# Attention scores and row maxima of two heads at a time as pairs of 64-row TensorE tiles, in a fused attention and FFN kernel

## The chip, the cores and the metric

One core of a Trainium2 chip. The metric is the device time of one execution in microseconds (us); the median of three runs of the kernel before is 858.36 us.

## The reference, cut to what matters

Attention with queries that are mean-pooled by two, and an FFN with a leaky activation behind it, all in float32:

```python
q_pool = q.reshape(B, H, S // 2, 2, D).mean(axis=3)      # B, H, S, D = 4, 8, 1152, 64
scores = np.matmul(q_pool, k.transpose(0, 1, 3, 2)) / np.sqrt(D)
scores = scores - np.max(scores, axis=-1, keepdims=True)
attn = np.exp(scores)
attn = attn / (np.sum(attn, axis=-1, keepdims=True) + 1e-09)
out = np.matmul(attn, v)                                  # 576 pooled queries in each of 32 heads
x = out.transpose(0, 2, 1, 3).reshape(B * S // 2, H * D)  # 2304 x 512
h = x @ w_in                                              # 512 -> 2048
g = np.maximum(h, 0.0) + alpha * np.minimum(h, 0.0)
return g @ w_out                                          # 2048 -> 512
```

## The kernel before, in words

**Order.** Every piece of work is a task for one engine with a planned cost and a priority; a list scheduler (`Scheduler`) writes the program of each engine out once, at build time. On the chip each engine takes its instructions in that order and waits on semaphores.

**Stages.** First the attention of 32 heads (to 453.5 us of the span), then the "low sweeps" (the first 5 of 16 blocks of the FFN's hidden units, in 8 blocks of 288 tokens, L474 with 288 columns), then the "high sweeps" (the other 11 blocks, 5 blocks of 460 or 464 tokens). The FFN's weights come as 64-bit floats and are converted by VectorE and ScalarE (five VectorE operations each, L386 to L422) as the work goes on; ten of the 32 half blocks of weights ahead of the last row maxima.

**Precision.** Numbers are split into a high part (type fp32r) and a low rest, and products are summed from high*high, high*low and low*high.

**One head of attention.** `head_prep` loads the keys twice, one copy under the other (64 + 64 partitions), and the summed queries likewise; `q1` holds high queries on partitions 0 to 63 and, from `q_low` (L739), low ones on 64 to 127, under which `k1` holds the high keys twice. One matmul with 128 rows so gives high*high plus low*high. `k2` holds low keys and a row of -1 (65 rows), `q2` high queries and the row maximum. The scores of a block of 128 keys and 288 queries are two matmuls (L983, L984) into one of three PSUM banks; ScalarE takes exp of each (L996). `head_max` finds the row maximum of the next head: 12 blocks of 128 queries and 384 keys (L911), two blocks to a double bank, one VectorE reduction over 768 columns for both (L927). The 64 queries that are left over (576 is 4.5 times 128) go as a block-diagonal tile `bd` against half keys `k3` (L892, L901). A TensorE transpose (L945) and a DMA bring the maxima into `q2`. Weighted values (L1024) are matmuls of plain float32, two 64-column tiles per key block, the two halves of the queries side by side. Sums of exp go over blocks: VectorE and GpSimd add blocks (L1009), TensorE sums what is left in 32-column tiles (L1046, per pair of heads, four parts per head for heads 0 to 11, two after), and `pair_end` normalises.

```python
pairs = [blocks[i:i + 2] for i in range(0, len(blocks), 2)]   # head_max: two blocks share a reduction
double[i] = (bank[i], bank[i + 1]), t                         # banks 3+4 and 5+6, for maxima alone
```

## Time and profile before

| what | value |
|---|---|
| timed runs | 858.26, 858.36, 858.57 us |
| profiled execution: its span, first to last instruction | 853.4 us |
| runs' median less that span | 4.96 us |
| TensorE busy | 841.0 us, 99% of the span, 5477 matmuls |
| VectorE busy | 583.0 us, 68% |
| ScalarE busy | 535.8 us, 63% |
| GpSimd busy | 193.1 us, 23% |
| first score matmul, last matmul of attention's sums | at 17.16 and at 453.51 us |

The profile gives no own total for the profiled execution beside its span; the 4.96 us lie outside the span. Matmuls overlap each other, so a busy TensorE is not yet TensorE at its pace: its pace is read from the starts of matmuls that follow each other.

### The profile page before, as it was taken

Reading aid. Unit: us, or ns where it says so; the run is one execution under the profiler, and the core shown is the slowest. Engines: PE = TensorE matmul, PEld = TensorE weight load, DVE = VectorE, ACT = ScalarE, POOL = GpSimd, SP = SyncE. Lnnn points to the kernel's source line nnn. Section 1 sums busy time; section 2 is a strip of 40 time slices with the busy share of each in tenths; the row PEclk is TensorE's granted clock in tenths of the full one; section 3 lists DMA queues with packets and bytes.
Section 4 is the critical chain, followed back from the end, with each engine's and each line's share of the span. In section 5 each row is a group of like instructions: output and inputs, shape, how many; then the busy total and the mean of one; then the engine's idle time right before and its main releaser. Section 6 shows DMA issues by size and latency. Waiting matters only on the chain.

```text
span 853.4 us, 14873 instructions
## 1 busy us (share of the span) xinstructions
PE 841.0 (99%) x5477; PEld 708.7 (83%) x5477; DVE 583.0 (68%) x897; ACT 535.8 (63%) x1295; POOL 193.1 (23%) x146
## 2 busy tenths in 40 slices
PE   8999999999999999999999999999999999999997
PEld 7777777767877877877879999998888888888886
DVE  7988999999989989989894699623332323322423
ACT  6888888889899899888764576534332233222321
POOL 4534333235534545534530000000000000000000
PEclk9999999999999999999999999999999999999999
DMA  8355754685565665643443867545330321300301
GB/s 299 113 132 148 231 163 143 213 230 151 152 175 124 178 157 142 169 119 95 113 117 116 252 208 246 169 136 167 88 90 4 100 76 44 89 1 1 90 0 46
DMA packets 71376, 112.74 MB, mean 132 GB/s; under 512 B 20779, under 2 KB 45958, under 8 KB 71302
## 3 DMA queue, kind: packets, MB, share of 16 engines
q1 hardware_dynamic: 69430, 104.12, 40.5%
q0 software_dynamic: 1872, 7.67, 5.2%
q8 instruction: 43, 0.70, 0.3%
q14 instruction: 31, 0.25, 0.1%
HBM read 92.65 MB, written 19.02 MB: 131 GB/s over the span
## 4 chain that ended last, share of the span: by engine, by line
PE 82%; DVE 9%; DMA 4%; ACT 3%; issue 1%; SPq 0%; DVEq 0%; ACTq 0%
PE bank L474 40%; PE bank L1024 13%; PE bank L983 9%; PE bank L984 8%; PE bank L911 7%; DMA wraw<-wt 3%; PE bank L1046 2%; DVE wbits L416 1%; ACT pa L996 1%; PE bank L892 1%; DVE bx L927 1%; DVE wbits L410 1%; DVE wmag L422 1%; PE bank L945 1%; DVE pa L1009 1%
## 5 line engine op out<-in xcount | busy, mean ns | idle before, releaser
L1009 POOL TENSOR_TENSOR pa<-pa,pa 128x576 f32<-128x576 f32 x116 | 170.4, 1484 | 226.3 <-ACT pa L996 208.9
L996 ACT ACTIVATE pa<-bank 128x288 f32<-128x288 f32 x576 | 201.7, 411 | 30.8 <-PE bank L984 25.7
L927 DVE TENSOR_REDUCE bx<-bank 128x2 f32<-128x768 f32 x194 | 175.9, 947 | 10.6 <-PE bank L911 9.4
L983 PE MATMUL bank<-q,k 128*128 128x288 f32 x576 | 169.2, 309 | 2.6 <-ACT pa L996 1.2
L984 PE MATMUL bank<-q,k 65*128 65x288 f32 x576 | 163.3, 297 | 0.0
L1024 PE MATMUL bank<-pa,vv 128*64 128x288 f32 x1152 | 149.2, 410 | 0.0
L1024 PEld LDWEIGHTS bank<-pa,vv 128*64 128x64 f32 x1152 | 78.8, 137 | 56.1 <-issue 7.2
L983 PEld LDWEIGHTS bank<-q,k 128*128 128x128 f32 x576 | 108.6, 189 | 14.1 <-ACT pa L996 4.7
L519 DVE TENSOR_TENSOR gw<-gs,gw 128x460 fp32r<-128x460 f32 (+1 forms) x55 | 35.1, 638 | 119.4 <-ACT gw L514 119.2
L514 ACT ACTIVATE gw<-gs 128x460 fp32r<-128x460 f32 (+1 forms) x55 | 32.4, 589 | 124.4 <-PE bank L474 115.2
L984 PEld LDWEIGHTS bank<-q,k 65*128 65x128 f32 x576 | 109.3, 190 | 0.0
L911 PE MATMUL bank<-k,q 128*128 128x384 f32 x372 | 96.2, 342 | 0.1
L474 PE MATMUL bank<-gw,wh 128*128 128x460 f32 (+1 forms) x320 | 93.4, 373 | 0.5
L474 PE MATMUL bank<-wlow,wh 128*128 128x460 f32 (+1 forms) x320 | 93.0, 371 | 0.0
L508 DVE SCALAR_TENSOR_TENSOR gs<-gs,nal 128x460 f32<-128x460 f32 (+1 forms) x55 | 38.4, 699 | 56.1 <-ACT gs L503 56.0
L498 ACT ACTIVATE gs<-bank 128x460 f32<-128x460 f32 (+1 forms) x55 | 30.2, 549 | 63.0 <-PE bank L474 62.2
L474 PEld LDWEIGHTS bank<-gw,wh 128*128 128x128 f32 x320 | 59.3, 188 | 9.5 <-DVE x L590 2.5
L474 PE MATMUL bank<-x,wlow 128*128 128x288 f32 x480 | 67.1, 295 | 0.0
L474 PE MATMUL bank<-gs,wlow 128*128 128x288 f32 x480 | 66.2, 296 | 0.6 <-DVE gs L519 0.6
L474 PEld LDWEIGHTS bank<-wlow,wh 128*128 128x128 f32 x320 | 60.1, 188 | 7.1
L474 PEld LDWEIGHTS bank<-gs,wlow 128*128 128x128 f32 x480 | 64.1, 188 | 2.1 <-DVE gs L519 1.4
L474 PEld LDWEIGHTS bank<-x,wlow 128*128 128x128 f32 x480 | 64.8, 188 | 0.5 <-issue 0.4
(101 smaller groups left out, 1204.2 us busy)
## 6 DMA issues: line engine op xcount, KB each, us to landing
kk<-kt SPq DMA_DIRECT2D x31, 576.0 KB
wraw<-wt SPq DMA_DIRECT2D x32, 512.0 KB
qs<-qt SPq DMA_DIRECT2D x19, 576.0 KB
vv<-vt SPq DMA_DIRECT2D x32, 288.0 KB
xs<-x SPq DMA_DIRECT2D x64, 144.0 KB
x<-xs SPq DMA_DIRECT2D x32, 288.0 KB
qs<-qt POOLq DMA_DIRECT2D x13, 576.0 KB, 8.0
r<-rrd SPq DMA_DIRECT2D x64, 72.0 KB
```

What stands on the lines that cost most here:

```text
L474: nc.tensor.matmul(out=ps[:, :n], lhsT=w[a, c // DMO][:, c % DMO:c % DMO + P], rhs=lo(hl), start=(first and i == 0), stop=(last and i == 2),)
L498: ACT, act(n, True), lambda: nc.scalar.activation(out=flat(pos), in_=ps.t[:, :n], func=AF.Relu),
L508: lambda: nc.vector.scalar_tensor_tensor(out=flat(pos), in0=flat(neg), scalar=nal[:, f:f + 1], in1=flat(pos), op0=ALU.mult, op1=ALU.add),
L514: ACT, act(n), lambda: nc.scalar.activation(out=gs.t[:, 0, :n], in_=flat(pos), func=AF.Copy),
L519: lambda: nc.vector.tensor_tensor(out=gs.t[:, 1, :n], in0=flat(pos), in1=gs.t[:, 0, :n].bitcast(F32), op=ALU.subtract),
L911: nc.tensor.matmul(out=ms.t[:, i, :JW], lhsT=(flat_of(raw, F32R) if raw else q1.t)[:, c:c + P], rhs=k1.t[:, j * JW:(j + 1) * JW], start=Tr ...
L927: lambda c=c, e=e, step=step, m=len(pair), ms=ms: nc.vector.tensor_reduce(out=bx.t.rearrange("p t j -> p (t j)")[:, c:e + 1:step], in_=ms. ...
L983: nc.tensor.matmul(out=ps.t[:, :HQ], lhsT=k1.t[:, s], rhs=q1.t[:, q], start=True, stop=False)
L984: nc.tensor.matmul(out=ps.t[:, :HQ], lhsT=k2[n % 2][:, s], rhs=q2[n % 2][:, PAD + q.start:PAD + q.stop], start=False, stop=True)
L996: lambda ps=ps, p=p, h=h: nc.scalar.activation(out=p.t[:, h], in_=ps.t[:, :HQ], func=AF.Exp, scale=SCALE),
L1009: lambda a=a, b=p, part=part, e=e: e.tensor_tensor(out=part.t, in0=a.t, in1=b.t, op=ALU.add),
L1024: nc.tensor.matmul(out=av.t[h * D:(h + 1) * D, :HQ], lhsT=vv.t[:, e], rhs=p.t[:, h], start=(e == 0), stop=(e == NC - 1),)
```

## The change

Heads are taken two at a time. `k1`, `k2`, `q1`, `q2` now hold head n on partitions 0 to 63 and head n+1 on 64 to 127, each once; nothing is stored twice. Scores of a block of 128 keys and 288 queries of both heads are eight matmuls of 64 rows (L948), in four pairs: high*high, low query*high key, high query*low key, and a tile of -1 (`neg`) against `mq`, a tile of zeros with the maxima in one row per head. The two matmuls of a pair use different halves of the array's rows and write two different PSUM banks. `half_main` is a pass over all keys for half of the queries of both heads, so one block of exp (`pa`) holds both heads; weighted values and sums follow that layout, and `vv` is needed of both heads. Row maxima are one 64-row matmul per block and head (L815), into a bank of its own, with a reduction of 384 columns each (L836); the 64 queries left over use two chained matmuls per piece (L822) against `rt`, a tile with zeros on both sides. Both heads share one transpose step (L852). The copies into `bd`, `k3` and `q2` are gone, as is the double load of queries and keys. The first pair loads both members of each query pair, sums them on VectorE (L740), and has the maxima of both heads ahead of its first score. Banks are single: at first five for scores and three for maxima (bank 6 in both lists), after the 14th pass seven for either and for low sweeps, any two free ones for a block of scores. Blocks of exp are weighted in one group of nine key blocks in all heads (before, in two groups for heads 0 to 11), and all heads have two parts of sums. A matmul with 64 rows and a full matmul are different modes for the scheduler. In the low sweeps some tasks are merged; their matmuls stay the same. Nine half blocks of weights are converted ahead of the last row maxima. Many of the scheduler's numbers differ too.

```diff
+                        s = max(s, self.free[eng])
+                        if eng == PE and self.col and not t.col:
+                            s += self.turn
+                        cand.append((s, t))
...
-    q0: bass.AP,
...
-    PB: int = 15,
...
+    PB: int = 13,
...
-    PL: int = 3,
...
+    PL: int = 0,
...
-    GROUPS: tuple = ((3, 8), (8,)),
...
+    GROUPS: tuple = ((8,), (8,)),
...
-    JH: int = 12,
...
+    JH: int = 0,
...
-    ADDS: tuple = ((3, 5, 6, 8), (2, 7, 8)),
...
+    ADDS: tuple = ((4, 6, 8), (6, 7, 8)),
...
-    EARLY: tuple = ((0, 1, 2), (3, 5), ()),
...
-    LATE: tuple = ((0, 1, 2), (3, 5), (0, 1, 2, 3, 5)),
...
+    EARLY: tuple = ((1, 2, 3, 4, 6), (0, 5, 6), ()),
...
+    LATE: tuple = ((0, 1, 2, 3, 4, 5, 6), (0, 1, 2, 3, 4, 5, 6), (1, 2, 3, 4, 5, 6)),
...
+        w.kk, w.k1, w.k2 = Buf(r_kk), Buf(r_k1), Buf(r_k2)
+        w.qs, w.q1, w.q2, w.rt = Buf(r_qs), Buf(r_q1), Buf(r_q2), Buf(r_rt)
...
+            lambda: e1.tensor_tensor(
+                out=w.q2.t, in0=qs.t, in1=w.q1.t.bitcast(F32), op=ALU.subtract
             ),
...
+        load_q(qc[0], -9)
+        load_k(kc[0], -8.9)
+        load_k(slice(JW, S), -8.8)
+        load_q(slice(2 * P, SQ), -8.7)
...
+        items = [(t, j) for t in range(NQT - 1) for j in range(NJ)]
+        rests = [(-1, 0), (-1, 1)]
+        items[BD:BD] = rests
+        if first:
+            items = [(t, j) for t in range(NQT - 1) for j in range(NJ)] + rests
+        items = [(t, j, i) for t, j in items for i in range(2)]
...
+            ms, d = Buf(r_ms), both[i]
...
+            def rows(t=t, j=j, d=d, ms=ms):
+                if t >= 0:
+                    nc.tensor.matmul(
+                        out=ms.t[:, :JW], lhsT=w.q1.t[d, t * P:(t + 1) * P],
+                        rhs=w.k1.t[d, j * JW:(j + 1) * JW], start=True, stop=True,
+                    )
+                    return
+                for u in range(2):
+                    c = (2 * j + u) * (S // 4)
+                    nc.tensor.matmul(
+                        out=ms.t[:, :S // 4], lhsT=w.rt.t[d, D - D * u:D - D * u + P],
+                        rhs=w.k1.t[d, c:c + S // 4], start=u == 0, stop=u == 1,
+                    )
...
+                nc.vector.tensor_reduce(out=bx.t[:, at, j:j + 1], in_=ms.t[:, :m], axis=AX.X, op=ALU.max)
...
+                nc.tensor.matmul(out=mt.t[i][:, :D], lhsT=mx.t[d], rhs=identr[d, d], start=True, stop=True)
...
-                    for i in range(2):
-                        nc.tensor.matmul(
-                            out=ms.t[:, i, :S // 4], lhsT=bd[n % 2], rhs=k3_b[n].t[:, i * S // 4:(i + 1) * S // 4],
-                            start=True, stop=True,
-                        )
...
-            def rows(pair=pair, ms=ms):
-                for i, (t, j) in enumerate(pair):
-                    c = t * P if raw else PAD + t * P
-                    nc.tensor.matmul(
-                        out=ms.t[:, i, :JW], lhsT=(flat_of(raw, F32R) if raw else q1.t)[:, c:c + P],
-                        rhs=k1.t[:, j * JW:(j + 1) * JW],
-                        start=True, stop=True,
-                    )
...
-                lambda c=c, e=e, step=step, m=len(pair), ms=ms: nc.vector.tensor_reduce(
-                    out=bx.t.rearrange("p t j -> p (t j)")[:, c:e + 1:step], in_=ms.t[:, :m, :JW],
-                    axis=AX.X, op=ALU.max,
-                ),
...
-                def scores(ps=ps, q=q, s=s):
-                    nc.tensor.matmul(out=ps.t[:, :HQ], lhsT=k1.t[:, s], rhs=q1.t[:, q], start=True, stop=False)
-                    nc.tensor.matmul(
-                        out=ps.t[:, :HQ], lhsT=k2[n % 2][:, s], rhs=q2[n % 2][:, PAD + q.start:PAD + q.stop], start=False, stop=True
-                    )
...
+            p, ps = Buf(r_p), Buf(r_ps)
...
+            def scores(ps=ps, s=s):
+                pairs = ((w.k1, w.q1), (w.k1, w.q2), (w.k2, w.q1), (None, w.mq))
+                for x, (k, r) in enumerate(pairs):
+                    for i, d in enumerate(both):
+                        nc.tensor.matmul(
+                            out=ps.t[i][:, :HQ], lhsT=k.t[d, s] if k else neg[d], rhs=r.t[d, q],
+                            start=x == 0, stop=x == len(pairs) - 1,
+                        )
...
+                    lambda ps=ps, p=p, i=i: nc.scalar.activation(
+                        out=p.t[:, i], in_=ps.t[i][:, :HQ], func=AF.Exp, scale=SCALE
                     ),
...
                         nc.tensor.matmul(
-                            out=av.t[h * D:(h + 1) * D, :HQ], lhsT=vv.t[:, e], rhs=p.t[:, h],
+                            out=av.t[i * D:(i + 1) * D, :HQ], lhsT=w.vv[i].t[:, e], rhs=p.t[:, i],
                             start=(e == 0), stop=(e == NC - 1),
...
+        single = [
+            ((bank[i],), psum.tile([P, 512], F32, tag=f"bank{i}", name=f"bank{i}")) for i in range(8)
+        ]
...
+            r_ps.places = [
+                (single[i][0] + single[j][0], (single[i][1], single[j][1])) for i in scores for j in scores if i < j
+            ]
+            r_ms.places = [single[i] for i in maxima]
+            r_h.places = r_y.places = [single[i] for i in hidden]
...
-        "qt": twice(q.reshape(B * H // 2, 2, S // 2, 2, D).transpose(0, 3, 4, 1, 2), 2),
-        "kt": twice(k.reshape(B * H, S, D).transpose(0, 2, 1), 1),
+        "qt": q.reshape(B * H // 2, 2, S // 2, 2, D).transpose(0, 3, 1, 4, 2).reshape(B * H // 2, 2, 2 * D, S // 2),
+        "kt": k.reshape(B * H // 2, 2, S, D).transpose(0, 1, 3, 2).reshape(B * H // 2, 2 * D, S),
...
-        "q0": q[0, 0].reshape(S // 2, 2, D).transpose(1, 2, 0).reshape(P, S // 2),
```

**TensorE, middle of the attention stage, before** (`k` and `q` in L911 are the next head's keys and queries; L983 and L984 write one score block into bank_119 to bank_121; bank_117 and bank_118 are the double banks):

```order
L911 MATMUL bank_117<-k_2886,q_2849 128x384 x2
L983 MATMUL bank_120<-q_2552,k_2589 128x288
L984 MATMUL bank_120<-q_1_109,k_1_107 128x288
L983 MATMUL bank_119<-q_2552,k_2589 128x288
L984 MATMUL bank_119<-q_1_109,k_1_107 128x288
L983 MATMUL bank_121<-q_2552,k_2589 128x288
L984 MATMUL bank_121<-q_1_109,k_1_107 128x288
L911 MATMUL bank_118<-k_2886,q_2849 128x384 x2
```

Between three score blocks of two matmuls stand two blocks of maxima of one head. The same place in the program of the change (bank_118 to bank_125 are banks 0 to 7; matmuls alternate between head n and head n+1):

```order
L815 MATMUL bank_118<-k_1870,q_1831 128x384
L815 MATMUL bank_123<-k_1870,q_1831 128x384
L948 MATMUL bank_119<-q_1501,k_1509 128x288
L948 MATMUL bank_120<-q_1501,k_1509 128x288
L948 MATMUL bank_119<-q_1883,k_1509 128x288
L948 MATMUL bank_120<-q_1883,k_1509 128x288
L948 MATMUL bank_119<-q_1501,k_1897 128x288
L948 MATMUL bank_120<-q_1501,k_1897 128x288
L948 MATMUL bank_119<-mq_112,neg 128x288
L948 MATMUL bank_120<-mq_112,neg 128x288
L815 MATMUL bank_124<-k_1870,q_1831 128x384
```

The eight matmuls of a score block stand together; blocks of maxima come between score blocks, here once as a pair and once one alone.

**VectorE, start of the program, before** (the first head's reductions, L927, the peak over blocks, L848, then the second head's low queries and maxima):

```order
L848 TENSOR_REDUCE mx_110<-bx 128x3
L927 TENSOR_REDUCE bx<-bank_117 128x2
L927 TENSOR_REDUCE bx<-bank_118 128x1
L1177 TENSOR_SCALAR nal<-nal 128x16
L848 TENSOR_REDUCE mx_110<-bx 128x2
L739 TENSOR_TENSOR q_267<-qs,q_267 64x576
L901 TENSOR_REDUCE mx_111<-bank_117 128x1
```

The first scores need what stands up to the second L848. In the change (L836 are the reductions of both first heads, L892 the peaks, L770 and L781 the low queries and keys, L921 the peak of the 64 queries left over; bx_114 belongs to the second pair):

```order
L836 TENSOR_REDUCE bx_113<-bank_124 128x1
L836 TENSOR_REDUCE bx_113<-bank_123 128x1
L1146 TENSOR_SCALAR nal<-nal 128x16
L892 TENSOR_REDUCE mx_107<-bx_113 128x10
L770 TENSOR_TENSOR q_397<-qs,q_185 128x576
L781 TENSOR_TENSOR k_400<-kk,k_189 128x512
L836 TENSOR_REDUCE bx_114<-bank_124 128x1
L921 TENSOR_REDUCE mq_111<-bank_118 1x64 x2
```

Ahead of the last L892 stand 28 reductions, those of both heads; low queries and the first low keys moved behind them, and the second pair's reductions begin there.

## Rows read from the trace of the kernel before

**Rows 1.** Page, span and TensorE: busy time, share of the span, matmuls.

```profile
span 853.4 us, 14873 instructions
PE 841.0 (99%) x5477; PEld 708.7 (83%) x5477; DVE 583.0 (68%) x897; ACT 535.8 (63%) x1295; POOL 193.1 (23%) x146
```

**Rows 2.** Windows, all engines: busy us (x instructions), PEclk, DMA share, GB/s.

```profile
150.00:250.00 100.00, 98.45 (x733) 75.54 (x731) 97.88 (x145) 89.04 (x225) 40.58 (x30) 1.00 0.66 181
250.00:400.00 150.00, 149.76 (x1126) 119.22 (x1123) 134.87 (x194) 133.59 (x337) 71.38 (x53) 1.00 0.57 148
```

**Rows 3.** Chain that ended last, sums of pairs: start us, us, what.

```profile
100.95 2.08 PE bank L1046 x32
...
214.08 1.11 PE bank L1046 x16
...
392.13 1.11 PE bank L1046 x16
```

**Rows 4.** Timeline of TensorE, end of a head: start us, us, what, count.

```profile
246.40 0.51 PE L911 MATMUL bank<-k,q 128*128 128x384 f32 x2
246.75 0.29 PE L983 MATMUL bank<-q,k 128*128 128x288 f32 x1
246.88 0.29 PE L984 MATMUL bank<-q,k 65*128 65x288 f32 x1
...
248.45 4.59 PE L1024 MATMUL bank<-pa,vv 128*64 128x288 f32 x36
252.97 0.33 PE L945 MATMUL bank<-identr,mx 128*128 128x128 f32 x1
253.13 0.35 PE L983 MATMUL bank<-q,k 128*128 128x288 f32 x1
```

**Rows 5.** Timeline of TensorE, sums of one pair of heads in 32-column tiles.

```profile
239.71 1.18 PE L1046 MATMUL bank<-pa,ones 128*32 128x288 f32 x16
240.82 0.33 PE L945 MATMUL bank<-identr,mx 128*128 128x128 f32 x1
```

**Rows 6.** Chain that ended last, weighted values in two groups.

```profile
92.94 2.09 PE bank L1024 x16
...
98.37 2.58 PE bank L1024 x20
```

**Rows 7.** Timeline of VectorE, one head: start us, us, what, count.

```profile
396.61 3.55 DVE L927 TENSOR_REDUCE bx<-bank 128x2 f32<-128x768 f32 x4
400.07 0.75 DVE L901 TENSOR_REDUCE mx<-bank 128x1 fp32r<-128x576 f32 x1
400.73 0.16 DVE L939 TENSOR_REDUCE mx<-bx 128x4 fp32r<-128x12 f32 x1
...
403.42 1.34 DVE L726 TENSOR_TENSOR k<-kk,k 64x1152 fp32r<-64x1152 f32 x1
404.69 0.41 DVE L404 TENSOR_SCALAR wbits<-wraw 128x512 int32<-128x512 int32 x1
```

**Rows 8.** Groups by form, VectorE: one of five operations of a weight conversion.

```profile
L410 DVE SCALAR_TENSOR_TENSOR wbits<-wraw,wbits 128x512 int32<-128x512 int32 x32 | 22.6, 708 | 0.3
```

**Rows 9.** Groups by form, ScalarE: exp, and copies of half keys.

```profile
L996 ACT ACTIVATE pa<-bank 128x288 f32<-128x288 f32 x576 | 201.7, 411 | 30.8 <-PE bank L984 25.7 <-issue 0.2
L653 ACT ACTIVATE k<-k 64x576 fp32r<-64x576 f32 x62 | 42.2, 681 | 0.7
```

**Rows 10.** Timeline of the start: the last part of the keys, VectorE, the first score.

```profile
6.85 0.94 ACT L780 ACTIVATE k<-kk 128x384 fp32r<-128x384 f32 x2 [0.86 <-DMA kk<-kt]
...
16.36 0.16 DVE L848 TENSOR_REDUCE mx<-bx 128x2 fp32r<-128x6 f32 x1
...
17.16 0.40 PE L983 MATMUL bank<-q,k 128*128 128x288 f32 x1
```

**Rows 11.** Groups by form, weight loads (PEld) of 128 and of 64 columns.

```profile
L983 PEld LDWEIGHTS bank<-q,k 128*128 128x128 f32 x576 | 108.6, 189 | 14.1 <-ACT pa L996 4.7 <-issue 2.0 <-ACT rs L1058 1.9
L1024 PEld LDWEIGHTS bank<-pa,vv 128*64 128x64 f32 x1152 | 78.8, 137 | 56.1 <-issue 7.2 <-DMA rc<-rsd 0.2 <-DMA r<-rrd 0.2
```

More of the change, by code (lines that the diff above doesn't have):

```diff
@@ L185, in run @@
                             key, pick, first = p, t, s
+                if eng == PE and self.col and not pick.col:
+                    first -= self.turn
                 if best is None or first < best[0]:
@@ L1164, in add_warm @@
             n = WN if sch.now < WT * 1000 else WM
-            add(PE, 430 if sch.now < WT * 1000 else 54 * n, lambda: warm(n), writes=[filler], prio=50, kind="warm")
+            add(PE, 58 * n, lambda: warm(n), writes=filler, prio=50, kind="warm", col=1)
         sch.free[PE] = WB
```

705 lines of the change are left out of this document (320 added, 385 removed).

## The prediction

> **What bounds the kernel now.** I read the page first. TensorE is busy for 99% of the span and no other engine for more than 68% [rows 1]. Its matmuls overlap, so the timeline has to say whether "busy" is "at its pace". In a steady stretch it is: score matmuls of 288 columns start 0.13 us apart (246.75 to 246.88; 0.134 in the mean), two maxima blocks of 384 columns take 0.35, 0.178 each (246.40 to 246.75), the 36 matmuls of weighted values 4.52 (248.45 to 252.97), the transpose 0.16 [rows 4]. For a head that is 36 x 0.134 + 12 x 0.178 + 2 x 0.134 + 4.52 + 0.16 + about 0.1 for the switch of mode ahead of the weighted values = 12.0 us. A pair is 24.0, and with its sums, 1.11 [rows 5], 25.1. The chain of waits shows what a pair takes: from 214.08 to 392.13 lie seven pairs, 25.4 us each [rows 3]. So from 214 us on TensorE waits for almost nothing.
>
> Between 100.95 and 214.08 a pair takes 28.3 us [rows 3], though its own work is only about 1.3 us longer there (sums of 2.08 in place of 1.11, and two groups of weighted values that take 2.09 + 2.58 in place of 4.52 [rows 6, 3]). The windows say who is late: VectorE is busy for 97.88 of 100 us from 150 on, and for 134.87 of 150 us from 250 on [rows 2]. That is the point to keep in mind: TensorE is the bound, and VectorE stands right behind it, at 90% where no weights are converted and at 98% where they are.
>
> **TensorE's work.** The terms, for the whole program:
>
> *Scores.* Before, 1152 matmuls, one at a time, 0.134 each. After, 2304 of 64 rows in 1152 pairs. If the two matmuls of a pair run side by side, a pair takes what one matmul took and the term is 0. No row of before shows tiles of 64 rows. The nearest rows are column tiles: 36 matmuls of two 64-column tiles take 4.52, 0.126 each; 16 matmuls of four 32-column tiles take 1.11 [rows 4, 5], 0.069 each, about half. The same 288 columns cost half when four share the array in place of two, so small tiles run side by side here. I take 0; the other end, one after the other, is 1152 x 0.134 = +154.
>
> *Row maxima.* Before, 387 matmuls of 0.178, 68.9 us. After, 384 of 64 rows, of which a pair again takes the time of one. They pair only where two stand together, one of each head. In the order some stand alone between score blocks and some in threes (the rows shown have a pair and one alone). I walked through it with two tiles, each matmul starting after the one ahead of it and when its tile is free: 221 slots. 221 x 0.178 = 39.3, so -29.5. The ends are -34.7 (all mated, 192 slots) and 0 (none).
>
> *Queries left over.* Before, 62 matmuls of 0.134, 8.3 us. After, 128, of which two are chained on one tile and then two on the other, so that four need about three slots, five where eight stand together: 85 slots, 11.4 us. +3.
>
> *Transposes.* 31 of 0.16 become 15 pairs of half the columns, with the first pair's own turn: -3.
>
> *Sums and groups, heads 0 to 11.* Six pairs have 16 sum matmuls in place of 32, 6 x (2.08 - 1.11) = -5.8, and eleven heads have one group of weighted values in place of two, 11 x (2.09 + 2.58 - 4.52) = -1.7 [rows 3, 4, 6]. Together -7.5.
>
> *Switches of mode.* Scores and maxima were full matmuls and are now one mode; weighted values leave and enter it as before. Low sweeps between scores now switch too, some five times at 0.1 to 0.2 us: +1. Low and high sweeps, about 400 us, do the same matmuls.
>
> Sum: 0 - 29.5 + 3 - 3 - 7.5 + 1 = **-36 us**, if nothing new waits.
>
> **The start.** The first score starts at 17.16, 0.8 us after the second peak of maxima [rows 10]. After the change all 28 reductions of both heads stand ahead of that peak, and low queries (0.67) and a piece of low keys (0.6) ahead of the first score. A reduction of 768 columns takes 0.865 (four from 396.61 to 400.07), one of 576 takes 0.66 (400.07 to 400.73) [rows 7]: 1.07 ns a column, so 0.455 for 384 and 0.352 for 288. The last keys land at 6.85 [rows 10]; copied, they let VectorE go on at about 7.3 with some 20 + 4 reductions, 10.5 us, the two low parts, 1.3, sums of queries, 0.5. That is 19.6, plus 0.8 to the first score and 0.5 for one more small peak and copies: 21. Twice the query bytes land ahead, up to 1 us. **+4.5**, between +2 and +8. TensorE has nothing else to do there.
>
> **VectorE.** Per pair of heads: reductions go from 12 x 0.865 + 2 x 0.66 = 11.7 to 24 x 0.455 + 4 x 0.352 = 12.3, +0.6. Subtractions for the low parts run on 128 partitions once, not on 64 twice: -1.27 (403.42 to 404.69 [rows 7]) and about -0.67, and one small peak and step less, -0.3. Net about -1.5. Before, 134.87/150 of 25.4 is 22.8 us busy; after, 21.3. TensorE's pair falls to 25.4 - 1.9 = 23.5 (maxima 24 x 0.178 less 14 slots, -1.8; rests +0.2; transposes -0.2). So without conversions VectorE needs 91%: it fits. But the order puts nine conversions of a half block between the second and tenth pair; each is four operations of 0.71 [rows 8] and one of 0.41 [rows 7], 3.2 us. There VectorE needs 24.5, and at 98% a pair takes 25.0, 1.5 longer than TensorE's, over some nine pairs +13. Before, the same cause cost 28.3 - 26.5 = 1.8 in five or six pairs, 10 us, which are won back. **Net +3**, between -3 and +20. A wait of this kind goes straight into the end: the matmul of a maxima block waits for a bank, and every score behind it on TensorE with it.
>
> ScalarE loses the copies of half keys (62 of 0.68 [rows 9]) and more, GpSimd gains 12 additions; ScalarE was 89% busy at most [rows 2], so nothing is gained. The second loads of keys and queries go; nothing on TensorE waited for them in a steady pair: 0.
>
> **Sum.** -36 + 4.5 + 3 = -28.5. On the profiled span, 853.4 - 28.5 = 825, and with 4.96 us outside it 830; on the median of the runs 858.4 - 28.5 is the same, 830. I take **829**, since some slots counted alone will find a mate in the score block behind.
>
> **The rivals.**
>
> *VectorE takes the bound.* At 91 to 104% of TensorE's new pair there is little left for waits. If it reaches only 90% of its time, as from 250 on, where TensorE left it no more work, pairs take 21.3/0.9 = 23.7 without and 24.5/0.9 = 27.2 with conversions. Against the 23.5 and 25.0 of the sum that is 6 x 0.2 + 9 x 2.2 = 21 us more, **850**; it decides about the sign at about 88%, where 9 x 2.8 + 6 x 0.7 = 29. For it: 98% busy already at 150 to 250 us. Against it: it held that 98%. The page "TensorEngine Tiling (Array Packing)" of the Trainium skill, section "PSUM Bottleneck", says that tiling speeds up TensorE but not the reading of PSUM, which may become the bottleneck; the window at 150 us agrees, and by that rule alone the time is this rival's.
>
> *Exps press the score banks.* A block of scores takes two banks for 0.54 us and two exps of 0.35 (201.7/576 [rows 9]). Per pair of heads 18 blocks have 23.5 - 9.04 = 14.5 us, 0.8 each, against 0.7 of ScalarE: 12% of room, before 22%. With two pairs of banks in turn at 0.9 us a block, 18 x 0.1 x 15 = +27 us at worst, about half of it likely: **842**.
>
> *Weights of a pair don't load side by side* (the other side). A load takes 189 ns for 128 columns and 137 for 64 [rows 11]: 0.81 ns a column, 104 ns for a tile of 128. Now one such load hides under each 0.134 of matmul. If the two loads of a pair follow each other, a pair takes 0.208 in place of 0.134: 1152 x 0.074 = +85 for scores, 306 x 0.03 or more for maxima and rests, +9: 858 - 28 + 94 = **924**. It decides from 0.159 us a pair on (28.5/1152 = 0.025 over 0.134). For it: no row shows two loads within 104 ns. Against it: two 64-column loads and matmuls in column tiles ride together without cost. The page "TensorE: Matmul & The Clock Gate" of the Trainium skill, section "LDWEIGHTS (loading the stationary operand)", says that the time of a load goes by columns, not rows, so halved rows save nothing; the trace's slope agrees. Its section on packing says that different row groups load and run at once, but measures 3.07 times for four row tiles; by an estimate from that, a pair would take 0.174, and the time would be some 46 us over my sum.
>
> *Nothing hidden is lost.* All maxima mated and VectorE keeping up: -36 - 5 + 3 = -38, **820**.
>
> **Chances.** Forecast 0.57 (822 to 837); VectorE 0.16; exps 0.07; loads or no overlap 0.08 (up to 858 - 28 + 154 = 984); better than the forecast 0.09; waits that just eat the gain 0.03. Range: from 813, which is the last rival without the loss at the start and a little under it, to 847, most of the way to VectorE's rival; it leaves out the loads' case and the far end of VectorE's. Faster by over 0.2% (1.7 us, what these runs, 0.3 us apart, can surely tell) is all but the last two groups: 0.89; the same 0.03; slower 0.08.
>
> **What would show it.** Two score matmuls of a pair starting within some 0.01 us, and pairs 0.134 apart: overlap holds; 0.2 apart: the loads. Maxima on TensorE near 39 us of slots. First score near 21.5. Pairs of heads from the eleventh on near 23.5 us, earlier ones near 25, VectorE near 95% in them. Sweeps unchanged at about 400 us. I am wrong if TensorE's idle time shows waits for L836 (VectorE) or L964 (exp) of more than some 15 us, or if a pair of matmuls costs more than 0.14.

## The result, and the profile after

The changed kernel takes **848.95 us** (median of 4 runs, 847.58 to 849.94), the kernel before 858.31 beside it (856.19 to 858.57): a ratio of 0.9893, 95% interval 0.9874 to 0.9911. The forecast was 829 with a range of 813 to 847. The sign was right; of 29 us forecast, 9.4 came. Its profiled run took 848.91 us, 847.1 of it span. The two lie some 1.8 us apart here and in every run that lists both, so the 4.96 us set against the kernel before are not all outside its span: its profiled execution was some 3 us shorter than its median, and the two traces lie 6.3 us apart where the medians lie 9.4.

The page after, span and engines, as in [rows 1]:

```profile
span 847.1 us, 17444 instructions
PE 833.1 (98%) x6686; PEld 695.8 (82%) x6686; DVE 574.5 (68%) x1071; ACT 436.4 (52%) x1124; POOL 207.3 (24%) x159
```

Windows after: two at the start, two within one half of a pair (scores, then weighted values), two as in [rows 2]. Behind a window's length stand the busy us of TensorE, of its weight loads, of VectorE, ScalarE and GpSimd, then the granted clock, the DMA share and GB/s.

```profile
23.00:26.00 3.00, 2.55 (x22) 1.11 (x18) 2.15 (x6) 0.96 (x2) 0.00 (x0) 0.50 0.00 0
26.00:30.00 4.00, 4.00 (x33) 3.78 (x31) 3.21 (x8) 1.96 (x6) 0.34 (x1) 0.50 0.78 237
...
225.50:232.10 6.60, 6.60 (x80) 5.84 (x76) 5.93 (x13) 6.08 (x18) 4.23 (x3) 1.00 0.10 31
232.10:236.60 4.50, 4.50 (x37) 2.50 (x36) 4.50 (x10) 2.61 (x7) 2.29 (x1) 1.00 0.35 131
...
150.00:250.00 100.00, 99.83 (x1047) 74.48 (x1046) 95.26 (x189) 67.67 (x188) 50.91 (x36) 1.00 0.46 140
250.00:400.00 150.00, 149.99 (x1596) 114.44 (x1598) 137.28 (x271) 98.55 (x282) 72.60 (x52) 1.00 0.34 97
```

ScalarE is busy for 98.55 of 150 us, 66%, well under the 89% of before. But in the score stretch it is 6.08 of 6.60, 92%, and then 2.61 of 4.50. VectorE is 90% and 100% busy in the same two stretches. Such shares alone don't show a bound: in a score stretch of the kernel before, where TensorE ran at its pace, the same two were at 96% and 90%:

```profile
240.90:248.40 7.50, 7.50 (x51) 7.29 (x51) 7.18 (x10) 6.78 (x20) 5.26 (x4) 1.00 0.45 133
```

The chain of waits after, the sums of the second, seventh, ninth, fourteenth and last pair of heads, as in [rows 3]; and one row of the kernel before that was not shown, the sums of its second pair:

```profile
79.95 1.11 PE bank L1013 x16
...
211.39 1.11 PE bank L1013 x16
...
262.00 1.11 PE bank L1013 x16
...
386.92 1.11 PE bank L1013 x16
...
453.10 1.11 PE bank L1013 x16
```

```profile
74.44 2.08 PE bank L1046 x32
```

From these rows and [rows 3], in us per pair of heads: pairs 3 to 7 took 27.9 before ((214.08 - 74.44)/5) and 26.3 after; pairs 8 to 14 took 25.44 before and **25.08** after. The forecast had 25.0 up to the tenth pair and 23.5 behind it.

The timeline of TensorE after, in a score stretch (start, duration, what, count):

```profile
225.25 0.29 PE L948 MATMUL bank<-mq,neg 64*128 64x288 f32 x2
225.38 0.51 PE L815 MATMUL bank<-k,q 64*128 64x384 f32 x3
...
226.26 0.74 PE L948 MATMUL bank<-q,k 64*128 64x288 f32 x6
226.71 0.43 PE L948 MATMUL bank<-mq,neg 64*128 64x288 f32 x2
```

Two 64-row score matmuls take 0.13 us together (225.25 to 225.38), as one full matmul did [rows 4]: the tiles do run side by side. But the three pairs from 226.26 to 226.71 take 0.45, not 0.39.

### The profile page after: what moved, and what is told of

It reads as the page before. It is cut to its first block, busy times and chain, and to the rows that moved or that the text cites. A ratio compares the mean times of both kernels' runs of the same rounds, so it can differ in the third digit from the quotient of the medians.

```text
span 847.1 us, 17444 instructions
## 1 busy us (share of the span) xinstructions
PE 833.1 (98%) x6686; PEld 695.8 (82%) x6686; DVE 574.5 (68%) x1071; ACT 436.4 (52%) x1124; POOL 207.3 (24%) x159
## 4 chain that ended last, share of the span: by engine, by line
PE 88%; DVE 5%; DMA 2%; issue 2%; ACT 2%; SPq 0%; DVEq 0%; ACTq 0%
PE bank L477 43%; PE bank L948 18%; PE bank L991 14%; PE bank L815 6%; PE bank L1013 2%; PE bank L1123 2%; PE bank L822 2%; DMA wraw<-wt 1%; DVE pa L977 1%; DVE bx L836 1%; DVE wbits L413 1%; DMA x<-xs 1%; DVE pos L513 0%; DVE wmag L425 0%; ACT neg L508 0%
## 5 line engine op out<-in xcount | busy, mean ns | idle before, releaser
L977 POOL TENSOR_TENSOR pa<-pa,pa 128x576 f32<-128x576 f32 x128 | 190.6, 1511 | 207.8 <-ACT pa L964 196.5
L836 DVE TENSOR_REDUCE bx<-bank 128x1 f32<-128x384 f32 (+1 forms) x448 | 216.0, 537 | 20.8 <-PE bank L815 14.8
L964 ACT ACTIVATE pa<-bank 128x288 f32<-128x288 f32 x576 | 196.7, 415 | 33.3 <-PE bank L948 23.1
L948 PE MATMUL bank<-q,k 64*128 64x288 f32 x1728 | 207.6, 314 | 0.2
L948 PEld LDWEIGHTS bank<-q,k 64*128 64x128 f32 x1728 | 162.7, 187 | 12.8 <-issue 4.4
L948 PE MATMUL bank<-mq,neg 64*128 64x288 f32 x576 | 114.3, 293 | 0.0
L815 PE MATMUL bank<-k,q 64*128 64x384 f32 x384 | 109.4, 366 | 1.9 <-DVE bx L836 1.6
L519 ACT ACTIVATE gw<-gs 128x460 fp32r<-128x460 f32 (+1 forms) x55 | 32.4, 589 | 126.7 <-PE bank L477 115.2
L977 DVE TENSOR_TENSOR pa<-pa,pa 128x576 f32<-128x576 f32 x96 | 84.0, 875 | 0.2
L948 PEld LDWEIGHTS bank<-mq,neg 64*128 64x128 f32 x576 | 82.6, 187 | 0.0
L815 PEld LDWEIGHTS bank<-k,q 64*128 64x128 f32 x384 | 62.3, 185 | 16.5 <-DVE bx L836 10.1
```

Source lines behind the costliest of these rows:

```text
L519: ACT, act(n), lambda: nc.scalar.activation(out=gs.t[:, 0, :n], in_=flat(pos), func=AF.Copy),
L815: nc.tensor.matmul(out=ms.t[:, :JW], lhsT=w.q1.t[d, t * P:(t + 1) * P], rhs=w.k1.t[d, j * JW:(j + 1) * JW], start=True, stop=True,)
L836: nc.vector.tensor_reduce(out=bx.t[:, at, j:j + 1], in_=ms.t[:, :m], axis=AX.X, op=ALU.max)
L948: nc.tensor.matmul(out=ps.t[i][:, :HQ], lhsT=k.t[d, s] if k else neg[d], rhs=r.t[d, q], start=x == 0, stop=x == len(pairs) - 1,)
L964: lambda ps=ps, p=p, i=i: nc.scalar.activation(out=p.t[:, i], in_=ps.t[i][:, :HQ], func=AF.Exp, scale=SCALE),
L977: lambda a=a, b=p, part=part, e=e: e.tensor_tensor(out=part.t, in0=a.t, in1=b.t, op=ALU.add),
```

## The experiments

Unless told otherwise an experiment is the changed kernel with one edit; ratios are to the kernel before, run beside it. Pairs of heads are worked out from chain rows like those above, "early" for pairs 3 to 7, "late" for 8 to 14; the changed kernel has 26.3 and 25.08. The versions with half reductions or half exps leave work out: they show what waits for what, and are no better kernels.

### Which reader of the banks holds TensorE up

Half reductions (each row maximum looks at half of the columns):

```diff
-  in_=ms.t[:, :m], axis=AX.X, op=ALU.max
+  in_=ms.t[:, :m // 2], axis=AX.X, op=ALU.max
```

> The changed kernel with its row-maxima reductions (L836) over the first half of each block's columns only (192 or 144 in place of 384 or 288), in an unchanged order on every engine; the maxima are then those of half the keys. It takes about 0.2 us from each of 448 VectorE operations, 5.5 us for a pair of heads. Theory A (TensorE's score blocks wait for ScalarE's exps to give their two banks back): pairs of heads stay at 24.5 us or more, the time at 842 to 849. Theory B (VectorE, 91 to 95% busy, sets the pair): pairs come near TensorE's own 23.2 to 23.6 us, the time falls to 822 to 832.

Half exps (half of the columns of a score block, with the other half of the slots filled ahead by GpSimd); then both edits:

```diff
-  out=p.t[:, i], in_=ps.t[i][:, :HQ], func=AF.Exp
+  out=p.t[:, i, :HQ // 2], in_=ps.t[i][:, :HQ // 2], func=AF.Exp
+  [nc.gpsimd.memset(s[1], 1.0) for s in slots]
```

> The changed kernel with exp (L964) over the first 144 of 288 columns of each score block; the other half of the blocks is set to one once at the start. Order unchanged on every engine but for those fills on GpSimd. It takes about 0.12 us from each of 576 ScalarE operations, 4.3 us for a pair of heads. Theory A (exps hold the score banks): pairs fall to 23.2 to 23.8 us, the time to 824 to 833. Theory B (VectorE sets the pair): pairs stay at 24.7 or more, the time at 843 to 849.

> Both cuts together, half the columns in the reductions and in the exps, order unchanged. If TensorE's own work was priced rightly (221 slots of maxima, a pair of matmuls as one, 23.2 us for a pair of heads), pairs come to 23.0 to 23.4 us and the time to 818 to 827 by either theory. If instead the pairs of matmuls cost more than I took, it stays at 835 or above.

In the half-exp run the fills made the first score 7.5 us late (33.69), so it was repeated without them, from the second pair on:

```diff
-  out=p.t[:, i], in_=ps.t[i][:, :HQ], func=AF.Exp
+  out=p.t[:, i, :HQ if n < 2 else HQ // 2], in_=ps.t[i][:, :HQ if n < 2 else HQ // 2], func=AF.Exp
```

> The changed kernel with its exps over half of the columns from the second pair of heads on (so the sums and weighted values use stale numbers in the other half; same work otherwise); no memory is set ahead, so the start is that of the changed kernel. Theory (two readers in turn): pairs of 24.3 to 24.6 late and 25 early, the time 6 to 10 us less, 839 to 843. Rival (ScalarE is a bystander, and the late pairs of 24.4 came from other work that the late start had shifted): pairs 25.2, the time 847 to 850.

Measured: half reductions 835.91 us, ratio 0.9746 [0.9728, 0.9764]; half exps with the fills 847.69, 0.9890 [0.9851, 0.9928]; half exps from the second pair 841.20, 0.9803 [0.9744, 0.9862]; both (with the fills) **826.91**, 0.9649 [0.9620, 0.9678]. Chain rows of half reductions, of half exps from the second pair, and of both, the second, seventh, ninth and fourteenth pair:

```profile
73.32 1.11 PE bank L1013 x16
...
199.99 1.11 PE bank L1013 x16
...
249.89 1.11 PE bank L1013 x16
...
373.38 1.11 PE bank L1013 x16
```

```profile
80.05 1.11 PE bank L1013 x16
...
208.32 1.21 PE bank L1013 x16
...
259.80 1.11 PE bank L1013 x16
...
381.67 1.11 PE bank L1013 x16
```

```profile
75.60 1.11 PE bank L1013 x16
...
196.74 1.18 PE bank L1013 x16
...
244.85 1.11 PE bank L1013 x16
...
362.99 1.11 PE bank L1013 x16
```

| | early | late | of these, pairs 10 to 14 |
|---|---|---|---|
| changed kernel | 26.3 | 25.08 | 24.98 |
| half reductions | 25.3 | 24.77 | 24.70 |
| half exps | 25.7 | 24.76 | 24.37 |
| both | 24.2 | **23.75** | **23.63** |

Late pairs lose 0.3 us with either edit alone and 1.3 with both. That is no sum of two costs: while one reader is late, relieving the other gives little. So neither of the two theories put up for the first two runs held by itself. The 0.3 of half exps is a mean: in pairs 10 to 14 they give 0.6, and in pairs 8 and 9 nothing (25.7 a pair, from 208.32 to 259.80, against 25.3), where the chain of that run goes through transfers of the sums (`rc<-rsd`, 5.71 us from 213.13 and 6.21 from 238.40). With both relieved the pair is close to the 23.5 that the forecast had for TensorE alone, so the forecast's prices of TensorE's work nearly hold, and what was missing lies in the two readers together.

The loads of weights show it directly. The load ahead of a score block waits for ScalarE's semaphore, one ahead of a maxima matmul for VectorE's. Counted in the traces over pairs 10 to 14 are those of these loads that start 0.03 to 0.07 us behind the end of an exp or of a reduction, and so were let go by it; behind the count stands the time since the load ahead of them, in sum, as far as it goes beyond a normal step of 0.134 us:

| | score loads let go by an exp: us | maxima loads let go by a reduction: us |
|---|---|---|
| kernel before | 57: 1.7 | 14: 0.2 |
| changed kernel | 78: 3.7 | 32: 3.5 |
| half reductions | 94: 6.7 | 19: 0.6 |
| half exps | 52: 0.5 | 38: 4.9 |
| both | 82: 1.2 | 20: 0.8 |

Relieving one reader moves the wait to the other: half reductions take 2.9 us of waits for reductions away and add 3.0 for exps. Both edits take away 5.2 of 7.2 us, where the five pairs became 6.8 shorter; the kernel before has 1.9. The sums are estimates: the 1.4 us that half reductions gained in these five pairs don't show in them.

Groups by form on TensorE, 250 to 400 us, scores (L948) and maxima (L815), of the changed kernel, half reductions, half exps from the second pair, and both; the last figure ahead of the second bar is the mean ns of one:

```profile
L948 PE MATMUL bank<-q,k 64*128 64x288 f32 x654 | 76.4, 310 | 0.0
...
L815 PE MATMUL bank<-k,q 64*128 64x384 f32 x142 | 40.6, 357 | 0.0
```

```profile
L948 PE MATMUL bank<-q,k 64*128 64x288 f32 x660 | 77.0, 312 | 0.0
...
L815 PE MATMUL bank<-k,q 64*128 64x384 f32 x130 | 33.8, 343 | 0.0
```

```profile
L948 PE MATMUL bank<-q,k 64*128 64x288 f32 x676 | 76.5, 302 | 0.0
...
L815 PE MATMUL bank<-k,q 64*128 64x384 f32 x139 | 40.9, 367 | 0.1
```

```profile
L948 PE MATMUL bank<-q,k 64*128 64x288 f32 x662 | 71.8, 301 | 0.0
...
L815 PE MATMUL bank<-k,q 64*128 64x384 f32 x125 | 32.9, 348 | 0.0
```

Relieving VectorE shortens the maxima and leaves the scores; relieving ScalarE shortens the scores and lengthens the maxima; only both shorten both. The idle column is 0.1 at most. A wait for a bank ends at the weight load ahead of the matmul, so it stands in a longer matmul, not in TensorE's idle time. The timeline of TensorE after shows such a score matmul, of 0.40 us in place of 0.29, and the timeline of its weight loads the load of the third maxima matmul ahead of it, let go at the same time:

```profile
227.29 0.40 PE L948 MATMUL bank<-q,k 64*128 64x288 f32 x1
```

```profile
227.29 0.18 PEld L815 LDWEIGHTS bank<-k,q 64*128 64x128 f32 x1 [0.26 <-DVE bx L836]
```

The load waited 0.26 us for a reduction, and the scores that stand behind it in TensorE's order waited with it.

### Can the readers be relieved without leaving work out

One exp of 576 columns for both heads' banks, order unchanged; the second version does so only where the two banks are neighbours:

```diff
-  nc.scalar.activation(out=p.t[:, i], in_=ps.t[i][:, :HQ], func=AF.Exp, scale=SCALE)
+  nc.scalar.activation(out=p.t, in_=every[:, i:j + 1:j - i, :HQ], func=AF.Exp, scale=SCALE)
```

> The changed kernel, with one exp of both heads' 576 columns per block of scores in place of two of 288; each engine's order is otherwise unchanged and nothing is left out. It relieves ScalarE alone, by the fixed part of one exp per block. Theory (TensorE waits in turn for two readers of its banks, VectorE and ScalarE, and either alone gives back a part): the steady pair falls from 25.3 to 24.5 to 24.9 and the time by 6 to 13 us, to 836 to 843; TensorE's score matmuls that start late behind an exp become fewer by half. Rival (VectorE alone sets the pair): the pair stays at 25.2 or more and the time within 2 us of 849. Rival (a block's banks come free as late as before, since the two banks are now let go together): no gain, or a loss.

> The changed kernel with one exp of 576 columns in place of two of 288 for the 210 of 288 blocks whose two banks stand next to each other, among them all from about 300 us on; where the banks lie apart (78 blocks, in the middle of the attention) there are two exps as before, so no wait through banks between them. The order of all work is unchanged and nothing is left out. Theory (TensorE waits for two readers in turn, ScalarE being the one that comes late in the score stretches): from 300 us on pairs fall from 25.0 to 24.4 to 24.7, in the first six from 25.4 to 25.2, and the time by 2 to 5 us, to 844 to 847. Rival (VectorE alone sets the pair, or both banks let go together are no sooner than one after the other): pairs at 25.0 or more, and 848 to 850.

Measured: 908.88 us, 1.0618 [1.0587, 1.0649], and with neighbours only 851.81, 0.9932 [0.9909, 0.9956]; both refute the gain. The first says nothing on exps: where a block's two banks lie apart, its strided access is taken to cover the banks between, so other matmuls waited for the exp; with neighbours only, TensorE's waits for maxima behind an exp are gone. The longest of its waits in the first run (what waits, for what; us in total, times, longest):

```profile
PE every L815 <- ACT pa L964: 19.3, 30, 1.0
```

The second is the fair test. Groups by form on ScalarE, 250 to 400 us, the exps of the changed kernel, then the joined ones:

```profile
L964 ACT ACTIVATE pa<-bank 128x288 f32<-128x288 f32 x218 | 74.5, 412 | 10.6 <-PE bank L948 7.8 <-ACT pa L964 0.6 <-PE bank L815 0.5
```

```profile
L964 ACT ACTIVATE pa<-every 128x576 f32<-128x576 f32 x41 | 26.6, 650 | 6.2 <-PE every L948 5.3 <-ACT pa L966 0.4 <-PE every L815 0.3
```

Two exps in a row keep ScalarE busy for 2 x 74.5/218 = 0.683 us, a joined one for 0.650. The edit relieves it by 33 ns a block, so there was next to nothing to gain, and it decides nothing about the readers.

One of VectorE's three additions per half moved to GpSimd, order unchanged:

```diff
-  e.tensor_tensor(out=part.t, in0=a.t, in1=b.t, op=ALU.add)
+  (nc.gpsimd if c == 6 else e).tensor_tensor(out=part.t, in0=a.t, in1=b.t, op=ALU.add)
```

> The changed kernel with one of the three additions of partial sums per half that VectorE does (the one of the seventh block of keys) done by GpSimd; the order is otherwise unchanged and nothing is left out. VectorE loses 2 x 0.87 = 1.75 us a pair of heads, half of what half reductions took from it (137.3 to 115.4 of 150 us, 3.7 a pair). Theory (VectorE, at 92 to 95%, holds TensorE up through the banks): pairs fall from 25.3 to about 24.9 to 25.1, and the time by 4 to 7 us, to 842 to 845. Rival (GpSimd's addition of 1.4 us is late for VectorE's next addition, and VectorE waits for it with the reductions behind): no gain, 849 or more.

Measured: 857.50 us, 1.0010 [0.9988, 1.0032], 8.5 more than the changed kernel: the rival. VectorE's wait from 50 to 400 us, which is missing in the changed kernel's list:

```profile
DVE pa L977 <- POOL pa L977: 8.5, 8, 1.3
```

VectorE's additions from 250 to 400 us, shortest, median and longest in ns, there and in the changed kernel:

```profile
L977 DVE TENSOR_TENSOR pa<-pa,pa x23: 694/752/2837, 250.9 to 390.8; 128x576 f32<-128x576 f32 x23
```

```profile
L977 DVE TENSOR_TENSOR pa<-pa,pa x36: 700/752/1935, 257.2 to 398.5; 128x576 f32<-128x576 f32 x36
```

A third of the additions went. The mean of those that stayed is 1019 ns, not 902, but the median is the same: what raises the mean is a few long ones, beside which GpSimd adds (see the last section). So VectorE lost less work than planned, and waited for GpSimd besides.

### The start

In the changed kernel the filling matmuls ended at about 17.6 us, the granted clock fell to 0.5 just behind 20, and the first score came at 26.22. First try, full-array fillers planned up to 21 us in place of 13.7, which plans the whole order anew; second, a 256-column filler behind each of the first pair's 28 maxima, order unchanged; third, the same with one exp per block:

> The changed kernel with filler matmuls up to 21 us of planned time in place of 13.7, as full 128-row matmuls into bank 7 alone; the scheduler then also places the first pair's second half of peaks behind its first scores, and orders later work somewhat differently. The granted clock fell to 0.50 from about 20 to 30.5 us and the first score started at 26.2. If that is worth what the rows say (half clock over 4 us of scores, turns and left-over blocks at 1.2 GHz ahead of them, and the late peaks), the first score starts near 21 to 22 and the time falls by 5 to 8, to 841 to 844. If the start hides behind VectorE anyway, 847 to 850.

> The changed kernel, with one more full-array filling matmul of 256 columns into the unused bank behind each of the first pair's 28 maxima matmuls; the order of all other work is unchanged and nothing is left out. In the changed kernel the granted clock fell to 0.50 from about 20 to 30.5 us, while TensorE had three or four matmuls in a microsecond, and the first score started at 26.22. If the low clock made the start late (the turns of the row maxima and the first scores run at half pace), the clock stays at 1.0, the first score starts near 24 and the time falls by 3 to 5 us, to about 845. If the start is late only because VectorE's 28 reductions and the low parts stand ahead of it, the first score stays near 26 and the time within 1.5 us of 849. If the fillers come in the way of the maxima, the first score is later than 26.5. The pairs later on should stay at 25.2 to 25.4 by either.

> Both edits together, the filling matmuls at the start and one exp per block of scores; nothing is left out. If the two act at different places, the gains add: 836 to 840 less 3 to 5 us for the start, about 834 to 839. If the start's gain is lost again in the first pairs, because VectorE has the same work to do by then, it is no faster than with one exp alone.

Measured: 856.70 (0.9986 [0.9966, 1.0007]), 864.96 (1.0102 [1.0074, 1.0129]) and 923.98 (1.0788 [1.0759, 1.0818]). All three missed: the first score came at 27.53, 38.87 and 41.29, since the fillers stood between maxima matmuls for which VectorE then waited. In the first the clock fell all the same (0.50 from 23 to 30 us); in the second it stayed at 1.00 up to 32 us and the start was far later. Fewer of them, in pairs of 64-row tiles, behind the last five maxima, the four left-over blocks and the turns; and the same with the moved addition, and with the exps of neighbouring banks joined:

```diff
+  def busy(k):
+      for y in range(k):
+          for i, d in enumerate(both):
+              nc.tensor.matmul(
+                  out=single[(7, 4)[i]][1].rearrange("p (a b) -> p a b", b=P)[:, :2], lhsT=even[d],
+                  rhs=even[d].unsqueeze(1).to_broadcast([D, 2, P]), start=True, stop=True,
+              )
...
+  busy(2 if first and x >= 19 else 0)
```

> The changed kernel with fewer and later filling matmuls than in the first try, which put them in the way: pairs of 64-row tiles of 256 columns, two pairs behind each of the first pair's last five maxima matmuls, one behind each of its four left-over blocks and two behind each of its two turns, into two banks that nothing uses by then. The order of all other work is unchanged, nothing is left out. If the granted clock of 0.50 from 20 to 30.5 us made the start late, the clock stays at 1.0, the first score moves from 26.2 to about 25, the scores up to 30 us run at full pace, and the time falls by 3 to 4 us, to 845 to 846. If only VectorE's work sets the start, the first score stays within 0.5 of 26.2 and the time within 1.5 us of 849.

> Both edits together, the later filling matmuls and the moved addition, as a version that may beat both kernels; nothing is left out. If they act at different places their gains add: 838 to 842. If VectorE's backlog is what the first pairs wait for anyway, the start's gain is lost there and it is no faster than with the moved addition alone.

> One exp for blocks with neighbouring banks and the later filling matmuls at the start together, nothing left out: a version that may beat both. The filling moved the first score 2 us forward and the first pair's sums 3.3, but at the last pair's sums nothing of it was left, since VectorE's conversions of weights stand in the way between 394 and 423 us. If that holds, this version is within 1.5 us of the one with one exp alone; if ScalarE's relief lets the gain through, it is 2 to 3 us faster than that.

Measured: 850.82 (0.9943 [0.9922, 0.9963]), 856.11 (0.9995 [0.9973, 1.0016]) and 850.07 (0.9922 [0.9898, 0.9946]). The later fillers did what they were for: from 26 to 30 us the window has a clock of 1.00 and 49 matmuls, not 33. The first score came at 24.23. And it gained nothing at the end. That kernel's window from 26 us:

```profile
26.00:30.00 4.00, 3.97 (x49) 3.60 (x50) 4.00 (x9) 3.06 (x11) 3.55 (x4) 1.00 0.83 268
```

Its chain, with the sums of the first, fourteenth and last pair and a part of what stands between:

```profile
50.80 1.11 PE bank L1024 x16
...
385.64 1.11 PE bank L1024 x16
...
419.88 1.81 DVE wbits L413
...
453.20 1.11 PE bank L1024 x16
```

The first pair's sums are 3.3 us sooner (the changed kernel's stand at 54.12 in its chain), the fourteenth's 1.3, the last 0.1 later. So 2.0 us of the lead were lost up to the fourteenth pair. Behind it the chain goes through VectorE's conversions of weights (L413 and others) and additions, in both kernels: the rest of the lead ends there.

No version that leaves nothing out is faster than the changed kernel.

### The kernel before

Its early pairs were put down to VectorE, and the shorter sums to the change. Half reductions; half exps from the third head on; and one group of weighted values and two partial sums for all heads, with the changed kernel's priority number for the sweeps (this last order is planned anew):

```diff
-  JH: int = 12,
+  JH: int = 0,
...
-  YL: float = 0.394,
+  YL: float = 0.337,
```

> The kernel before, with its reductions over half of the columns (so its row maxima are those of half of the keys, the rest of the work the same); the order is unchanged. It tells what of the kernel before VectorE holds up. The changed kernel gained 13 us from the same edit. If the early pairs of the kernel before, 28.0 to 28.6 us, are long because of VectorE, as the prediction has it, they fall to 26.5 to 27 and the time by 8 to 12 us, to 846 to 850; the later pairs, at TensorE's own pace, stay at 25.2 to 25.4. If it is ScalarE, or the order itself, they stay at 28 and the time falls by less than 3 us.

> The kernel before, with its exps over half of the columns from the third head on (stale numbers in the other half, the rest of the work the same), the order unchanged. Half reductions left its early pairs at 28. If ScalarE, busy for 89 to 90% there, holds TensorE up in the early pairs, they fall to about 27 and the time by 4 to 7 us, to 850 to 853. If the 28 us are TensorE's own (two groups, longer sums, more switches of mode between shorter stretches), they stay within 0.3 and the time within 2 us of 857.

> The kernel before, full matmuls, with two of the change's side edits alone: all heads have one group of weighted values and two partial sums each (in place of heads 12 to 15 only), and the priority number of the sweeps' second layer is that of the changed kernel. Nothing is left out. The prediction gave the groups and sums 7.5 us of the gain. If that term holds by itself, pairs in the first six fall from about 28 to 27 and the time to about 851; the sweeps then show whether their 4 us of unforecast gain come from the priority number. If VectorE sets the early pairs of the kernel before, the shorter sums give nothing there (28.0 to 28.4 a pair as before) and the time stays at 856 to 858.

Measured: 853.18 (0.9970 [0.9949, 0.9991]), 852.72 (0.9941 [0.9914, 0.9968]) and 866.16 (1.0126 [1.0079, 1.0173]). The window of the half reductions from 150 us, against [rows 2]:

```profile
150.00:250.00 100.00, 98.81 (x739) 75.96 (x740) 81.97 (x146) 90.12 (x227) 39.54 (x29) 1.00 0.66 181
```

The chain of the same run, sums of the second and seventh pair:

```profile
73.83 2.08 PE bank L1046 x32
...
212.84 1.11 PE bank L1046 x16
```

VectorE falls from 97.88 to 81.97 of 100 us, and pairs 3 to 7 take 27.8 against 27.9. VectorE's reductions were not what they waited for. Half exps brought pairs 3 and 4 from 27.29 (74.44 to 129.01) to 26.77 (73.74 to 127.28), and by the starts of their sums pairs 3 to 6 from 27.8 to 27.3: ScalarE held some 0.5 us of these pairs. But pair 7 took 32.4 there against 28.6, with the chain in transfers of the sums' reciprocals (`r<-rrd`, 5.11 us from 199.32), so that pairs 3 to 7 together were not faster (28.3 against 27.9). The version with shorter sums has pair 3 at 25.3 (80.06 to 105.40) against 26.5, about what sums and groups are worth; in all, with its new order, it is 9 us slower, and what is the order's and what the groups' was not separated.

## Why the prediction was wrong

**Scores, 0 us: right as work.** 0.13 a pair of matmuls. The rival that the loads go one after the other (924) is refuted.

**Maxima -29.5, left-over queries +3, transposes -3: right, as work.** Time between starts in the timeline, added up by kind over pairs 8 to 14: maxima 30.16 before and 15.79 after, left-over 3.76 and 5.82, transposes 2.13 and 0.92. For 16 pairs that is -33, +4.7 and -2.8.

**The step that failed is "So without conversions VectorE needs 91%: it fits".** It set the mean busy share of one reader against TensorE's pair, and priced the other reader's press as a rival of its own; of ScalarE the sum said only that nothing is gained. Over the same seven pairs scores rose from 71.03 to 82.03 us, and took back 11 of the 14.4 that the maxima gave; with both readers relieved they take 75.2. Each bank has to be read before TensorE can write it again; in the score stretch ScalarE is 92% and VectorE 90% busy, TensorE waits for whichever comes last, and either relieved alone gives back 0.3 of the 1.3 us. The two rivals "VectorE takes the bound" (850) and "exps press the score banks" (842) are one cause. That 850 is nearly the time measured is luck: that rival had pairs of 27.2 with conversions and 23.7 without, and the runs have 26.3 early and 25.08 late, with a start 4.7 us later than its own. The sign that the prediction named, idle time of TensorE, stayed silent: waits for L836 are 2.5 us in the whole run, and there are none for L964, since the waits stand in longer matmuls. The page "TensorEngine Tiling (Array Packing)" of the Trainium skill, section "PSUM Bottleneck", says that tiling speeds up TensorE and not the reading of PSUM; the runs agree, for both readers: 23.75 a pair with both relieved.

**VectorE's work, -1.5 a pair: not all of it came.** The same 36 additions from 250 to 400 us keep VectorE busy for 26.8 us before and 32.5 after, some 0.95 a pair, which the term left out: after the change they often run beside an addition of GpSimd, before the change one of them did.

**"Before, the same cause cost 28.3 - 26.5 = 1.8 in five or six pairs" is refuted.** 98% busy was not the bound: half reductions left those pairs at 27.8. Of the excess over 25.4 the sums take 0.97, the two groups 0.3 and exps about 0.5; some 0.7 is not settled. The chain of the kernel before passes there through transfers of weights (`wraw<-wt`, 4.91 us from 147.03 and 6.84 from 173.18), which no run relieved, so they may be part of it.

**The start: +9.1, not +4.5.** The mechanism was right: half reductions brought the first score from 26.22 to 22.44, so all of their time may be worth up to twice that (an estimate), most of the 9.1. The size was wrong: the 28 reductions run from 8.28 to 23.32, 15.0 us, where 10.5 from 7.3 on were forecast. Those of 384 columns start 0.55 apart, not 0.455, and all 28 are behind that point, not 24. The term also left out the clock. The timeline of TensorE after, a turn of the maxima and the first scores:

```profile
25.27 1.02 PE L904 MATMUL bank<-ident,mx 128*1 128x128 f32 x8 [0.45 <-ACT mq L915]
26.22 1.09 PE L948 MATMUL bank<-q,k 64*128 64x288 f32 x6
```

The turns and the first scores ran at 0.5 of the clock, at 1.2 GHz, after TensorE had had three or four matmuls in a microsecond; with fillers in between it stayed at 2.4 GHz and the first score came 2.0 us sooner. By that run the clock costs nothing at the end.

**Sums and groups -7.5:** the sums fell from 2.08 to 1.11 us, as counted. That the shorter list bought time in the whole is not shown: the one run of it had a new order besides.

**Sweeps unchanged: not quite.** Windows from 600 to 840 us, before and after:

```profile
600.00:840.00 240.00, 239.59 (x1143) 213.60 (x1142) 74.71 (x113) 73.25 (x143) 0.00 (x0) 1.00 0.19 52
```

```profile
600.00:840.00 240.00, 240.00 (x1151) 215.69 (x1150) 73.93 (x112) 72.32 (x141) 0.00 (x0) 1.00 0.19 52
```

8 matmuls of 0.21 us more fit in, some 1.7 us. The kernel before with the new priority number and the shorter sums has 1150 there, so that number is the likely cause; it was not changed alone.

**The sum.** Against the forecast: start 4.7 late; pairs 3 to 14 took 386.92 - 79.95 = 307.0, where eight of 25.0 and four of 23.5 make 294, 13 more; from there to the end of the span 460.2, against 461.3 before less two pairs of 1.9, 2.7 more. That is 8.6 more in the last two pairs (386.92 to 453.10, 66.2, against 392.13 to 453.51, 61.4, less 3.8), about 3 of it 24 matmuls of the low sweeps that came forward, with the conversions that end last there; and 5.9 less behind them. Together 20, the miss on the medians. The traces, 6.3 us apart, miss some 2 more, which by subtraction lies in the first two pairs.

## What to carry to other kernels

When a change speeds up the engine that bounds a kernel, look at each engine that frees its buffers within the stretch where it does so, not at its share of the whole: ScalarE stood at 66% and still held TensorE up. Price such partners together, since relieving either alone gave 0.3 us of a pair and both gave 1.3. And no share shows a bound: with VectorE at 98%, halving its reductions gave the kernel before 0.1 us of a pair, and ScalarE's 90% of a score stretch cost little before the change and more after it. Take something of the partner's work away, or see which loads it lets go.

## What the runs showed of the hardware

- A wait for a bank doesn't show as TensorE's idle time: idle beside L948 is 0.0 while its matmuls lengthen from 301 to 310 ns in the mean.
- Back-to-back exps hide most of their fixed part. One of 288 columns takes 0.412 us and one of 576 takes 0.650, so the fixed part is some 0.17 (an estimate from the two). Two of 288 in a row keep ScalarE busy for 0.683, 0.033 more than the one of 576. The page "Perfetto Trace Analysis" of the Trainium skill, section "Optimizing Scalar/DVE Operations", gives some 51 ns of busy overhead for a ScalarE instruction that reads PSUM, and says that larger operations help a saturated engine; the 33 ns here are of that size, too small to help.
- An addition of GpSimd makes VectorE's additions beside it slower. From 50 to 400 us of the changed kernel they take 0.75 us in the mean where it overlaps under 5% of them (53 of 84) and 1.22 where it overlaps 30% or more (19); with the moved addition 0.75 (28) and 1.42 (20). Reductions that read PSUM take 0.55 either way. The same section says that shifting work between these two might not help since they share a port; that run agrees.
